# Four attention layers on one core: layers interleaved by superblocks under a build-time list scheduler

## The chip, the cores and the metric

The kernel runs on one core of a Trainium2 chip. The metric is the device time of one execution in microseconds (us), as the median of several runs. The engines are TensorE (PE in the rows; PEld is its weight load), VectorE (DVE), ScalarE (ACT), GpSimd (POOL) and SyncE (SP, which here only issues transfers).

## The reference

A sequence of 2,048 tokens of width 512 goes through four residual layers A, B, A, B. Both types have 32 heads of width 16. A is softmax attention over a sliding window of 256 keys; B is linear attention without a mask. The two A layers share their weights, and so do the two B layers.

```python
def _A_ref(x, wqkv, wo):                      # H = 32, Dh = 16, W = 256
    scores = jnp.einsum("bhqd,bhkd->bhqk", q, k) * (Dh ** -0.5)
    mask = (idx[:, None] - idx[None, :] >= 0) & (idx[:, None] - idx[None, :] < W)
    p = _softmax(jnp.where(mask[None, None], scores, -1e9), axis=-1)
    o = jnp.einsum("bhqk,bhkd->bhqd", p, v)
...
def _B_ref(x, wqkv, wo):
    phi = lambda t: jnp.where(t > 0, t + 1, jnp.exp(t)) + 1e-6
    pq, pk = phi(q), phi(k)
    kv = jnp.einsum("bhsd,bhse->bhde", pk, v)
    z = jnp.einsum("bhsd->bhd", pk)
    num = jnp.einsum("bhqd,bhde->bhqe", pq, kv)
    den = jnp.einsum("bhqd,bhd->bhq", pq, z)[..., None] + 1e-6
...
x = x + _A_ref(_layernorm(x, axis=-1), A_wqkv, A_wo)
x = x + _B_ref(_layernorm(x, axis=-1), B_wqkv, B_wo)
x = x + _A_ref(_layernorm(x, axis=-1), A_wqkv, A_wo)
x = x + _B_ref(_layernorm(x, axis=-1), B_wqkv, B_wo)
```

## The kernel before

The 2,048 tokens are 16 tiles of 128 rows, and four tiles make a superblock `I` of 512 queries. The residual `xres` stays on the chip in float32, the weights in bfloat16. `network` runs the four layers one after the other (`layer_A`, `layer_B`, each with its own PSUM pools).

**Layer A.** `prep_units` (L202) normalises a superblock's tiles: statistics on VectorE (L160, L162), the reciprocal root on GpSimd (L164, L166), the normalised tile on VectorE, ScalarE or GpSimd (L173, L178, L180), then a transpose by DMA from SP's queue (L215) or on TensorE (L186). Projections are four matmuls of 128x512 each: queries (L221), keys (L232), values (L245). The keys go to `kb` twice, with even and with odd heads masked out, so that one 32-row matmul makes the scores of a pair of heads for 64 keys; 16 pairs fill 32 heads. A row group is the quarter of TensorE's rows that a pair uses (pair modulo 4). Values go through `vst` and four small DMAs into the block-diagonal `vbd`.

`scores` (L276) treats a group of pairs (`GROUPS`: four of three pairs, two of two) and a bin of two runs of four windows (a window is 64 queries against 64 keys): matmuls (L286) into one of two PSUM buffers of three banks (`psA`), one exponential on ScalarE for up to 1,536 columns (L298), then triangular masks on GpSimd (L308) into one of nine buffers `pt`. Superblocks 1 to 3 have five bins (`BINS`), superblock 0 four (`BINS0`). `pv_pair` (L318) multiplies the masked exponentials with `vbd`, 24 matmuls of 34 columns per pair (18 in superblock 0); the 17th column of each head sums the row. `finalize` (L327, L329) divides. `outproj_units` (L268 to L272) transposes by DMA, multiplies by `wo` and adds the residual.

The order in A is written out by hand: while the scores of superblock `I` run, the projections of `I + 1` and the outputs of `I - 1` are dealt out between the score phases. Behind a layer, the row sums are tested (L387 to L393); where they are out of range, a slow version of the network runs after the fast one. It doesn't run here.

**Layer B.** For each tile LN, keys (L426), values (L432), and phi as an exponential on ScalarE and two passes on VectorE (L403 to L405); the products of keys and values of all 16 tiles add up in PSUM (`kvacc`, L441). Query projections (L447) follow per superblock. Only when all tiles are in, `kvbd` is made (L464, L466), and a second loop runs numerators and denominators (L474), the division (L478 to L481), a DMA transpose (L484), the output projection (L490) and the residual (L493, L496) for each tile.

The framework places every instruction on its engine's queue in the order of this code with some reordering by priority, and each engine works its queue in order.

Of the kernel before, what the change touches and what calls it, by code (L numbers as in the profile page):

```python
# [31 lines left out]
R1 = [(7, 7, 1), (-2, 0, 3)]  # L32
R2 = [(5, 5, 3), (-4, 0, 1)]
R3 = [(1, 1, 3), (0, 4, 1)]
R4 = [(3, 3, 3), (2, 6, 1)]
R5 = [(0, 0, 4)]
R6 = [(2, 2, 4)]
R7 = [(-1, 0, 4)]
R8 = [(4, 4, 4)]
R9 = [(-3, 0, 2), (6, 6, 2)]  # L40
R10 = [(1, 4, 2), (3, 6, 2)]
BINS = [(R3, R4), (R5, R6), (R1, R2), (R7, R8), (R9, R10)]
BINS0 = [(R3, R4), (R5, R6), (R8, R10), ([(5, 5, 3)], [(7, 7, 1), (6, 6, 2)])]
GROUPS = [(0, 1, 2), (3, 4, 5), (6, 7, 8), (9, 10, 11), (12, 13), (14, 15)]


def bin_windows(bins):

    win = {u: [] for u in range(4)}
    for b, runs in enumerate(bins):  # L50
        for r, run in enumerate(runs):
            pos = 0
            for (j, w0, n) in run:
                w = w0
                if w % 2:
                    assert pos == 0
                    win[w // 2].append((b, r, -1, j))
                    w += 1
                while w + 1 < w0 + n:
                    win[w // 2].append((b, r, pos + w - w0, j))  # L60
                    w += 2
                if w < w0 + n:
                    assert pos + w - w0 == 3
                    win[w // 2].append((b, r, pos + w - w0, j))
                pos += n
    return win


def bin_masks(runs):

    found = {}
    for r, run in enumerate(runs):
        pos = 0
        for (j, w0, n) in run:
            for w in range(w0, w0 + n):
                if w - j in (0, 4):
                    found.setdefault((w - j, pos + w - w0), []).append(r)
            pos += n
    return [(k, pos, rs) for (k, pos), rs in sorted(found.items())]
# [3 lines left out]
def build(ctx, tc, A_x, A_wqkv, A_wo, B_x, B_wqkv, B_wo, out, layers="ABAB", force_safe=False):  # L83
    nc = tc.nc
    S = A_x.shape[-2]
    NT, NSS = S // P, S // 512

# [3 lines left out]
    small = ctx.enter_context(tc.tile_pool(name="small", bufs=6))  # L91
# [34 lines left out]
    def load_weights():  # L126
        if w_loaded[0]:
            return
# [63 lines left out]
    def layer_A(x_old, x_new, w, wo, a_idx):  # L192
# [9 lines left out]
        def prep_units(I):  # L202
# [56 lines left out]
            for t in range(NCT):  # L259
                units += [qproj(t), kproj(t)]  # L260
# [410 lines left out]
```

## Time and profile before

| | us |
|---|---|
| median of 3 runs | 603.53 (601.71 to 605.83) |
| profiled execution | 602.24 |
| its span, first to last instruction | 600.2 |
| TensorE busy in it | 460.0 (77%), mean granted clock 0.892 |
| ScalarE busy | 367.5 (61%) |
| VectorE busy | 332.5 (55%) |
| GpSimd busy | 272.1 (45%) |

A busy time is the union of the instructions on an engine, so that an average over the whole span mixes stages that wait for different things. TensorE's matmuls are pipelined and their ends are modelled: the step from one start to the next tells more than a duration. The granted clock of TensorE is given as a share of 2.4 GHz; its two levels are 1.0 (2.4 GHz) and 0.5 (1.2 GHz).

### The profile page before, as it was taken

To read this page: it belongs to the slowest core of one execution; us is meant where nothing else is said; L and a number is where in the kernel's file an instruction comes from. 1 tells how busy PE (TensorE), PEld (TensorE's weight loads), DVE (VectorE), ACT (ScalarE), POOL (GpSimd) and SP (SyncE) were. 2 spreads that over 40 slices of the span, in tenths; PEclk is the share of its full clock that TensorE was granted. 3 is DMA by queue.
4 is the path that set the end of the run, shared out by engine and by line. 5 is a ranking of instruction groups with operands and counts; after the bars stand their busy time and mean duration, and the time that the engine had idled before them with its cause. 6 is when DMAs were issued, how large, how long until landed. Compare 5 with 4: busy or idle time off the path is not lost. (4 is left out here: it accounts for less than half of the span.)

```text
span 600.2 us, 15126 instructions
## 1 busy us (share of the span) xinstructions
PE 460.0 (77%) x6032; PEld 250.1 (42%) x6114; DVE 332.5 (55%) x729; ACT 367.5 (61%) x373; POOL 272.1 (45%) x667
## 2 busy tenths in 40 slices
PE   0178888888878879995647788888887887899573
PEld 0133455545546534452213345554544553444231
DVE  7731546545623365777886154554562336677773
ACT  1557679799779824660025857988978892466000
POOL 9444457657556562200035435675755666320000
PEclk9996899999976678997988779899998788999787
DMA  9412115031020030211431211501302103021363
GB/s 302 127 27 60 16 37 75 2 48 30 2 64 11 3 80 10 41 31 35 72 70 36 57 19 34 78 2 42 35 2 53 24 2 76 14 44 29 74 120 92
DMA packets 83375, 29.66 MB, mean 49 GB/s; under 512 B 67936, under 2 KB 82784, under 8 KB 83296
## 3 DMA queue, kind: packets, MB, share of 16 engines
q1 hardware_dynamic: 78256, 23.88, 19.9%
q10 hardware_dynamic: 5040, 4.72, 2.6%
q8 instruction: 50, 0.82, 0.6%
q14 instruction: 29, 0.24, 0.1%
HBM read 6.29 MB, written 2.10 MB: 14 GB/s over the span
## 5 line engine op out<-in xcount | busy, mean ns | idle before, releaser
L298 ACT ACTIVATE pt<-A 128x1536 bf16<-128x1536 f32 (+1 forms) x228 | 281.0, 1321 | 52.9 <-PE A L286 46.3
L308 POOL TENSOR_SCALAR_AFFINE_SELECT pt<-pt 128x384 bf16<-128x384 bf16 (+3 forms) x456 | 184.3, 430 | 140.1 <-ACT pt L298 136.1
L318 PE MATMUL O<-vbd,pt 128*128 128x34 bf16 x2880 | 108.4, 182 | 27.7 <-POOL pt L308 22.7
L318 PEld LDWEIGHTS <-pt 128*128 128x128 bf16 x2880 | 89.8, 99 | 64.8 <-POOL pt L308 37.9
L286 PE MATMUL A<-qT,kb 32*128 32x192 bf16 (+3 forms) x1920 | 96.7, 249 | 17.1 <-ACT pt L298 14.6
L286 PEld LDWEIGHTS <-kb 32*128 32x128 bf16 x1920 | 50.1, 98 | 69.6 <-issue 64.3
L490 PE MATMUL py<-woB,oT 128*128 128x512 bf16 x124 | 39.3, 448 | 16.6 <-DMA oT<-ob 14.1
L327 DVE RECIPROCAL rall<-O 128x24 f32<-128x24 f32 (+1 forms) x48 | 13.8, 288 | 66.7 <-PE O L318 66.7
L164 POOL TENSOR_SCALAR ln_ve<-ln_mv 128x1 f32<-128x1 f32 x64 | 14.0, 225 | 69.7 <-DVE ln_mv L162 68.2
L221 PE MATMUL pq<-xnT,wA 128*128 128x512 bf16 x108 | 37.3, 432 | 9.2 <-DVE ln_stats L160 5.6
L271 PE MATMUL py<-woA,oT 128*128 128x512 bf16 x108 | 33.1, 397 | 14.1 <-DMA oT<-o_sb 12.4
L160 DVE BATCH_NORM_STATS2 ln_stats<-xres 128x6 f32<-128x512 f32 x64 | 42.5, 681 | 0.8
L235 DVE TENSOR_SCALAR kb<-pk,mask_even 128x512 bf16<-128x512 f32 x32 | 25.3, 791 | 28.6 <-PE pk L232 24.4
L232 PE MATMUL pk<-xnT,wA 128*128 128x512 bf16 x116 | 36.5, 414 | 5.0 <-ACT kb L237 2.5
L403 ACT ACTIVATE phi_e<-pkb 128x512 bf16<-128x512 f32 x32 | 19.1, 598 | 32.9 <-PE pkb L426 31.4
L166 POOL TENSOR_TENSOR ln_rstd<-ln_ve,mhalf 128x1 f32<-128x1 f32 x64 | 36.8, 582 | 4.3 <-ACT xn L178 0.4
L226 DVE CAST qT<-pq 128x512 bf16<-128x512 f32 x24 | 16.6, 691 | 33.5 <-PE pq L221 33.4
L432 PE MATMUL pvb<-wB,xnTb 128*128 128x512 bf16 x124 | 34.8, 395 | 0.2
L426 PE MATMUL pkb<-wB,xnTb 128*128 128x512 bf16 x122 | 34.0, 396 | 0.5 <-issue 0.4
L272 DVE TENSOR_TENSOR xres<-py,xres 128x512 f32<-128x512 f32 x32 | 22.0, 686 | 21.4 <-PE py L271 20.5
L245 PE MATMUL pv<-wA,xnT 128*128 128x512 bf16 x114 | 31.9, 380 | 2.2 <-ACT kb L237 0.8
L178 ACT ACTIVATE xn<-xres,ln_nmr,ln_rstd 128x512 bf16<-128x512 f32 x12 | 9.6, 827 | 37.9 <-DVE ln_nmr L176 37.9
(71 smaller groups left out, 522.0 us busy)
## 6 DMA issues: line engine op xcount, KB each, us to landing
vbd<-vst SPq DMA_DIRECT2D x128, 34.0 KB, 1.9
out_dram<-ost ACTq DMA_DIRECT2D x16, 128.0 KB, 1.9
wB<-in_B_wqkv_dram SPq DMA_DIRECT2D x1, 1536.0 KB, 11.2
xst<-in_A_x_dram SPq DMA_DIRECT2D x8, 128.0 KB, 2.6
wA<-in_A_wqkv_dram SPq DMA_DIRECT2D x2, 512.0 KB, 7.2
xst<-in_A_x_dram ACTq DMA_DIRECT2D x8, 128.0 KB, 4.0
wA<-in_A_wqkv_dram ACTq DMA_DIRECT2D x1, 512.0 KB, 4.3
woA<-in_A_wo_dram ACTq DMA_DIRECT2D x1, 512.0 KB, 8.2
```

Of the source, the lines that this page charges most:

```text
L160: nc.vector.bn_stats(stats[:], x_ap)
L166: nc.gpsimd.tensor_tensor(rstd[:], ve[:], mhalf[:], op=ALU.pow)
L221: nc.tensor.matmul(pq[:], lhsT=w[:, c, t * P:(t + 1) * P], rhs=xnTs[I][:, c, :], start=(c == 0), stop=(c == NCT - 1))
L232: nc.tensor.matmul(pk[:], lhsT=w[:, c, D + t * P:D + (t + 1) * P], rhs=xnTs[I][:, c, :], start=(c == 0), stop=(c == NCT - 1))
L271: nc.tensor.matmul(py[:], lhsT=oT[:, c, :], rhs=wo[:, c, :], start=(c == 0), stop=(c == NCT - 1))
L286: nc.tensor.matmul(A[:, g, r, pos:pos + n, :], lhsT=kbs[m // 8][32 * rg:32 * rg + 32, t, m % 8, :, :], rhs=qTs[I][32 * rg:32 * rg + 32, t, ...
L298: nc.scalar.activation(body[:, 0:2 * ng, 0:n, :], A[:, 0:ng, :, 0:n, :].rearrange("p g r s c -> p (g r) s c"), ACT.Exp, scale=0.25)
L308: nc.gpsimd.affine_select(out=v, in_=v, compare_op=ALU.is_ge, fill=0.0, base=1 if kind == 0 else -2, pattern=[[0, nx], [2 * s, 64]], chann ...
L318: nc.tensor.matmul(O[:, u, g, :, :], lhsT=PTs[b][:, s0:s0 + 2, :], rhs=vbd[(m // 8) % NV][:, m % 8, :, grp[g], :], start=(n == 0), stop=(n ...
L426: nc.tensor.matmul(pk[:], lhsT=xnT[:, c, u * P:(u + 1) * P], rhs=w[:, c, D:2 * D], start=(c == 0), stop=(c == NCT - 1))
L432: nc.tensor.matmul(pv[:], lhsT=xnT[:, c, u * P:(u + 1) * P], rhs=w[:, c, 2 * D:3 * D], start=(c == 0), stop=(c == NCT - 1))
L490: nc.tensor.matmul(py[:], lhsT=oT[:, c, :], rhs=wo[:, c, :], start=(c == 0), stop=(c == NCT - 1))
```

## The change

`layer_A`, `layer_B` and the hand-written order go. In their place `fast_network` describes all operations of all four layers to a `Planner`, each with an assumed cost per engine, what it reads and writes, the buffers it takes from rings, and a priority. `Planner.run` then walks through an assumed time at build: it picks again and again the operation that can start first (with a bias on some second engine, and a higher priority where starts are equal), puts it on that engine and emits its instructions. The result is a fixed order of each engine's queue. Evictions from PSUM, masks and normalisations may go to either of two engines.

The layers are interleaved by superblocks: as soon as superblock `I` of A is out, LN, key, value and query projections and the key-value sums of B for it may run, beside A's attention of the later superblocks; the sums are now added in SBUF by VectorE, tile pairs at a time (`kv_unit`). Behind the last superblock `kv_final` masks the sums; B's second half for superblock `I` is then followed by the next A of that superblock. Denominators get a matmul group and one reciprocal of their own for four tiles (`den_unit`).

Runs of windows are longer: five runs of eight windows instead of ten of four, so that a run is a whole bank. Score phases alternate between one buffer of three banks and one of two; the other three banks (`psM`, two before) serve all other matmuls. Groups are five of three pairs and one of a single pair. The `pt` buffers are five of each size. Masks may run as a multiplication with a triangle (`tri`) on VectorE. The key eviction writes both masked copies in one instruction per half. `x` is read from the loaded bfloat16 tile without a cast. Transposes go through TensorE in the first superblock, around the layers' ends and for every second tile of the last stage, and by DMA from SP's queue elsewhere. The stores of the result move from ScalarE's queue to SP's. The slow version gets its own layer B.

```diff
-BINS = [(R3, R4), (R5, R6), (R1, R2), (R7, R8), (R9, R10)]
-BINS0 = [(R3, R4), (R5, R6), (R8, R10), ([(5, 5, 3)], [(7, 7, 1), (6, 6, 2)])]
-GROUPS = [(0, 1, 2), (3, 4, 5), (6, 7, 8), (9, 10, 11), (12, 13), (14, 15)]
...
+RA = [(1, 1, 5), (-3, 0, 2), (-4, 0, 1)]
+RB = [(3, 3, 5), (-2, 0, 3)]
+RC = [(-1, 0, 4), (4, 4, 4)]
+RD = [(5, 5, 3), (0, 0, 5)]
+RE = [(7, 7, 1), (6, 6, 2), (2, 2, 5)]
+
+BINS = ([RA, RE, RB], [RD, RC])
+BINS0 = ([RD, RE], [[(1, 1, 5), (4, 4, 2)], [(3, 3, 5), (4, 6, 2)]])
+GROUPS = [(0, 1, 2), (3, 4, 5), (6, 7, 8), (9, 10, 11), (12, 13, 14), (15,)]
...
+def phases_of(bins):
+
+    n3, n2 = len(bins[0]), len(bins[1])
+    out = []
+    for grp in GROUPS:
+        u3 = [(b, p) for b in range(n3) for p in grp]
+        u2 = [(b, p) for b in range(n3, n3 + n2) for p in grp]
+        while u3 or u2:
+            for us, n in ((u3, 3), (u2, 2)):
+                if us:
+                    out.append((n, us[:n]))
+                    del us[:n]
+    return out
...
+        n = 0
+        while ready:
+            best = None
+            for o, t in ready.items():
+                ok = True
+                for s in o.takes:
+                    f = s.ring.free_at()
+                    if f is None:
+                        ok = False
+                        break
+                    t = max(t, f[0])
+                if not ok:
+                    continue
+                for e, c in o.cost.items():
+                    c, bias = c if isinstance(c, tuple) else (c, 0.0)
+                    start = max(t, free[e])
+                    key = (round(start + bias, 2), o.prio, o.n)
+
+                    if best is None or key < best[0]:
+                        best = (key, o, e, start, c)
...
+                if not is_warm(start):
+                    c *= {"scores": 1.6, "pv": 1.28}.get(o.kind, 2.0)
...
+            o.fn(e)
...
+        ps3 = pool("ps3", 1, space=PSUM)
+        ps2 = pool("ps2", 1, space=PSUM)
+        psM = pool("psM", 3, space=PSUM)
...
+        rings = {"M": Ring(3), "3": Ring(1), "2": Ring(1), "xnT": Ring(3), "xn": Ring(4), "oT": Ring(4), "ost": Ring(3),
+                 "phi": Ring(2), "pks": Ring(3), "vs": Ring(3), "ln": Ring(8), "rden": Ring(2)}
...
+            return pl.op({"DVE": .69, "ACT": (.6, actb)}, fn, EV, reads=reads, writes=writes, deps=deps, use=[take_slot] + list(use))
...
+            ap = pl.op({"DVE": .45} if first else {"POOL": 1.0, "DVE": (.6, 0.0 if fast else .8)}, f_ap, prio, reads=[B("x", i)],
...
+            mm = pl.op({"PE": .33}, f_mm, prio, reads=reads, deps=lastmm + list(bPT.r), take=[s], kind="scores")
...
+                        pc = .18 + .064 * c if y - x == 1 else len(ps) * (.18 + .064 * 1.25 * (y - x))
+                        o = pl.op({"POOL": pc, "DVE": (.1 + .064 * .75 * c, .3)}, f_m, prio, deps=[exo])
...
+                def fe(e, jj=jj, t=t):
+                    if i == 0:
+                        nc.vector.tensor_copy(kvs[jj][:], t["t"][:])
+                    else:
+                        nc.vector.tensor_tensor(kvs[jj][:], t["t"][:], kvs[jj][:], op=ALU.add)
+                pl.op({"DVE": .42}, fe, EV, deps=[o], use=[s], writes=[B("kvs", jj)])
...
+        for k in range(NH):
+            nc.gpsimd.memset(vbd[k][:], 0.0)
+        for k in range(NPT):
+            nc.gpsimd.memset(pts[3][k][:, 0:28:9, :], 0.0)
+            nc.gpsimd.memset(pts[2][k][:, 0:19:9, :], 0.0)
...
+        def prep(key, I, prio, actb=ACTB):
+            for t in range(NCT):
+                k_unit(key, I, t, prio)
+                q_unit(key, I, t, prio, actb)
+            for u in range(4):
+                v_unit(key, I, u, prio, actb)
+
+        def b_proj(key, I, prio, actb=ACTB):
+            for u in range(4):
+                bk_unit(key, 4 * I + u, prio)
+                bv_unit(key, 4 * I + u, prio, actb)
+                if u % 2:
+                    kv_unit(4 * I + u - 1, prio)
+            for t in range(NCT):
+                bq_unit(key, I, t, prio + .5)
+
+        for a in range(2):
+            for I in range(NI):
+                ka, kb_ = ("A", a, I), ("B", a, I)
+                lastI = I == NI - 1
+                if a == 1:
+                    R = den_unit(I, 1.5 if I < 2 else 2.5)
+                    for u in range(4):
+                        p2_tile(4 * I + u, R, 1.5 if I < 2 else 2.5, by_pe=I < 2, actb=0.0 if I < 2 else ACTB)
+                for u in range(4):
+                    ln_tile(ka, 4 * I + u, a == 0, 2, by_pe=(I == 0 or (a == 1 and I == 1)), actb=0.0 if I == 0 else ACTB, fast=I == 0)
+                prep(ka, I, 2.2, actb=0.0 if I == 0 else ACTB)
+                attention(I, 0)
+                out_A(I, a, 1.6 if lastI else 3, by_pe=lastI, actb=0.0 if lastI else ACTB)
+                for u in range(4):
+                    ln_tile(kb_, 4 * I + u, False, 1.6 if lastI else 3.2, by_pe=lastI, actb=0.0 if lastI else ACTB, fast=lastI)
+                b_proj(kb_, I, 1.8 if lastI else 4, actb=0.0 if lastI else ACTB)
+            kv_final(0)
+            check_sums(a)
+        for I in range(NI):
+            R = den_unit(I, 2)
+            for u in range(4):
+                p2_tile(4 * I + u, R, 2, by_pe=True if u % 2 == 0 else False, final=True, actb=0.0)
+        late_consts()
+        plan_log = []
+        with tc.manual_schedule():
+            span = pl.run(plan_log)
```

## Rows read from the trace of the kernel before

**Rows 1.** The page's first part: busy time, share of the span, instructions.

```profile
PE 460.0 (77%) x6032; PEld 250.1 (42%) x6114; DVE 332.5 (55%) x729; ACT 367.5 (61%) x373; POOL 272.1 (45%) x667
```

**Rows 2.** Windows by stage: length; busy of PE, PEld, DVE, ACT, POOL; clock, DMA.

```profile
0.00:41.10 41.10, 11.18 (x63) 5.12 (x65) 28.41 (x65) 15.19 (x24) 26.30 (x55) 1.00 0.54 166
41.10:211.20 170.10, 141.53 (x2519) 83.49 (x2550) 75.67 (x145) 143.69 (x122) 99.13 (x249) 0.88 0.16 31
211.20:326.70 115.50, 89.04 (x491) 41.20 (x500) 85.05 (x209) 36.22 (x60) 30.03 (x73) 0.88 0.25 49
326.70:497.10 170.40, 140.92 (x2519) 83.28 (x2550) 75.56 (x145) 143.89 (x122) 99.05 (x249) 0.88 0.17 31
497.10:600.20 103.10, 77.32 (x444) 36.99 (x451) 67.82 (x165) 28.56 (x48) 17.64 (x41) 0.90 0.31 65
```

**Rows 3.** Windows: two within the first attention, one within layer B's projections.

```profile
80.00:120.00 40.00, 33.73 (x657) 20.28 (x664) 22.11 (x44) 35.59 (x30) 26.22 (x64) 1.00 0.25 42
160.00:211.20 51.20, 42.49 (x809) 26.68 (x815) 17.61 (x36) 44.91 (x38) 30.30 (x81) 0.73 0.10 23
...
240.00:256.00 16.00, 15.89 (x88) 7.90 (x89) 11.52 (x24) 10.06 (x17) 3.55 (x9) 1.00 0.21 42
```

**Rows 4.** Waits, whole span: engine and line, released by; us in total, times, longest.

```profile
ACT pt L298 <- PE A L286: 46.3, 57, 4.4
...
PE O L318 <- POOL pt L308: 22.7, 35, 2.5
```

**Rows 5.** Groups by shape: exponentials, masks; busy us, mean ns, idle before by releaser.

```profile
L298 ACT ACTIVATE pt<-A 128x1536 bf16<-128x1536 f32 x144 | 198.7, 1488 | 21.3 <-PE A L286 17.4 <-POOL pt L308 3.8
...
L298 ACT ACTIVATE pt<-A 128x1024 bf16<-128x1024 f32 x72 | 71.9, 1033 | 21.6 <-PE A L286 20.1 <-POOL pt L308 1.3
...
L308 POOL TENSOR_SCALAR_AFFINE_SELECT pt<-pt 128x192 bf16<-128x192 bf16 x128 | 43.8, 357 | 38.2 <-ACT pt L298 36.8 <-PE py L271 1.4
...
L308 POOL TENSOR_SCALAR_AFFINE_SELECT pt<-pt 128x128 bf16<-128x128 bf16 x64 | 17.9, 294 | 15.4 <-ACT pt L298 15.4
```

**Rows 6.** Timeline in attention: start us, duration, engine, line, operation, count.

```profile
101.02 0.40 PE L286 MATMUL A<-qT,kb 32*128 32x256 bf16 x6
...
101.34 0.67 PEld L318 LDWEIGHTS <-pt 128*128 128x128 bf16 x24 [0.21 <-issue]
```

**Rows 7.** Timeline in layer B: two projections in a row.

```profile
259.12 1.02 PE L426 MATMUL pkb<-wB,xnTb 128*128 128x512 bf16 x4
...
259.98 1.03 PE L432 MATMUL pvb<-wB,xnTb 128*128 128x512 bf16 x4
```

**Rows 8.** Groups by shape: LN, transposed eviction, residual and phi's exponential.

```profile
L160 DVE BATCH_NORM_STATS2 ln_stats<-xres 128x6 f32<-128x512 f32 x64 | 42.5, 681 | 0.8
...
L166 POOL TENSOR_TENSOR ln_rstd<-ln_ve,mhalf 128x1 f32<-128x1 f32 x64 | 36.8, 582 | 4.3 <-ACT xn L178 0.4
...
L272 DVE TENSOR_TENSOR xres<-py,xres 128x512 f32<-128x512 f32 x32 | 22.0, 686 | 21.4 <-PE py L271 20.5 <-PE A L286 0.9
...
L403 ACT ACTIVATE phi_e<-pkb 128x512 bf16<-128x512 f32 x32 | 19.1, 598 | 32.9 <-PE pkb L426 31.4 <-PE kvacc L441 1.0 <-DVE pks L405 0.5
...
L164 POOL TENSOR_SCALAR ln_ve<-ln_mv 128x1 f32<-128x1 f32 x64 | 14.0, 225 | 69.7 <-DVE ln_mv L162 68.2 <-DVE vint L622 1.1
L173 DVE TENSOR_SCALAR xn<-xres,ln_mv,ln_rstd 128x512 bf16<-128x512 f32 x24 | 13.6, 567 | 18.6 <-DMA xnT<-xn 16.1 <-POOL pt L308 1.2 <-PE pT L186 1.1
...
L190 DVE COPY xnTb<-pT 128x512 bf16<-128x512 bf16 x4 | 1.6, 393 | 1.5 <-PE pT L186 1.5
```

**Rows 9.** One line's instructions: count, least/median/greatest ns, first and last start.

```profile
L404 DVE TENSOR_SCALAR phi_e<-phi_e x64: 260/294/709, 217.3 to 555.7; 128x512 bf16<-128x512 bf16 x64
...
L180 POOL TENSOR_SCALAR xn<-xres,ln_rstd,ln_nmr x28: 772/772/1284, 108.9 to 540.3; 128x512 bf16<-128x512 f32 x28
```

**Rows 10.** Group of the zeroing of vbd; timeline of SP's queue in the last stage.

```profile
L153 POOL MEMSET vbd<- 128x2176 bf16 x4 | 7.6, 1910 | 0.0
...
559.08 32.00 SPq L484 DMA_TRANSPOSE oT<-ob  x16
```

More of the change, by code (lines that the diff above doesn't have):

```diff
@@ L66, in bin_windows @@
[L66 to L72, printed above, removed]
+    for b, run in enumerate(bins):
         pos = 0
         for (j, w0, n) in run:
[L75 to L79 removed]
+            w = w0
+            if w % 2:
+                assert pos == 0
+                win[w // 2].append((b, -1, j))
+                w += 1
+            while w + 1 < w0 + n:
+                win[w // 2].append((b, pos + w - w0, j))
+                w += 2
+            if w < w0 + n:
+                assert pos + w - w0 == 7
+                win[w // 2].append((b, pos + w - w0, j))
+            pos += n
@@ new lines, in bin_windows, with bin_masks @@
+    return win
+def bin_masks(run):
+    found = {}
+    pos = 0
+    for (j, w0, n) in run:
+        for w in range(w0, w0 + n):
+            if w - j in (0, 4):
+                found.setdefault(w - j, []).append(pos + w - w0)
+        pos += n
+    return {k: tuple(v) for k, v in found.items()}
+def phases_of(bins):
[10 more added lines that the diff above has]
+    return out
@@ new lines, with __init__, free_at @@
+class Buf:
+    def __init__(self):
+        self.w, self.r = [], []
+class Ring:
+    def __init__(self, n):
+        self.n, self.tiles = n, [None] * n
+    def free_at(self):
+        b = [(0.0 if t is None else t.end + .1, k) for k, t in enumerate(self.tiles) if t is None or not t.left]
+        return min(b, default=None)
+class Slot:
+    def __init__(self, ring):
+        self.ring, self.users, self.left, self.end = ring, [], 0, 0.0
+class Op:
+    def __init__(self, n, cost, fn, prio, kind):
+        self.n, self.cost, self.fn, self.prio, self.kind = n, cost, fn, prio, kind
+        self.deps, self.slots, self.takes = set(), [], []
+        self.after = 0.0
+        self.end = None
@@ L183, in pe_transpose @@
-    def pe_transpose(dst, src, pool, tag, use_act=False):
-        pT = pool.tile([P, NCT, P], BF, name="pT", tag=tag)
+    vflags = consts.tile([1, 2], F32, name="vflags")
+    nc.vector.memset(vflags[:], 1.0)
+    tri = {k: consts.tile([P, 64], BF, name=f"tri{k}") for k in (0, 4)}
+    for k, t in tri.items():
+        nc.gpsimd.memset(t[:], 1.0)
+        nc.gpsimd.affine_select(out=t[:], in_=t[:], compare_op=ALU.is_ge, fill=0.0, base=1 if k == 0 else -2,
+                                pattern=[[2 if k == 0 else -2, 64]], channel_multiplier=-1 if k == 0 else 1)
@@ new lines, in safe_network @@
+    def safe_network():
+        with ExitStack() as ctx_l:
+            sx = ctx_l.enter_context(tc.tile_pool(name="sx", bufs=2))
+            for i in range(NT):
+                xst = sx.tile([P, D], BF, name="xst_s", tag="xst_s")
+                nc.sync.dma_start(xst[:], x_dram[i])
+                nc.vector.tensor_copy(xres[:, i, :], xst[:])
+        for li in range(4):
+            with ExitStack() as ctx_l:
+                if li % 2 == 0:
+                    layer_A_safe(ctx_l, xres, xres, wA, woA)
+                else:
+                    layer_B_safe(ctx_l, xres, xres, wB, woB, li == 3)
```

1032 lines of the change are left out of this document (607 added, 425 removed).

## The prediction

> **What bounds the kernel now.** The page's busy line comes first: no engine is above 77% and ScalarE, VectorE and GpSimd lie between 45% and 61% [rows 1]. Nothing is full over the whole, so the span has to be cut into stages. I cut it where the exponentials of line 298 begin and end; the table of windows then shows five stretches [rows 2]: 41.1 us before the first exponential, two attention stretches of 170.1 and 170.4 us, 115.5 us between them (layer B, then the projections of the second layer A) and 103.1 us behind them (the second B). Attention is 340.5 us, everything else 259.7 us.
>
> In attention ScalarE is the engine to watch: 143.7 of 170.1 us, 84%. In an inner window at granted clock 1.00 it is 35.59 of 40 us, 89%, with TensorE at 33.73 [rows 3]. What ends its waits is the score matmul (46.3 us in both stretches), while TensorE's PV matmuls wait for GpSimd's masks (22.7 us) [rows 4]. In the non-attention stretches ScalarE is nearly idle (36.2 of 115.5 us) and TensorE does 89.0 us of work, dense only in places: 15.89 of 16 us in the projections of B [rows 2, 3]. Two stage types with different bounds run one after the other; the change runs B's projections under A's exponentials.
>
> **The change part by part.** *Exponentials.* The columns stay: 16 pairs x (30 + 3 x 40) windows x 64 = 153,600 a layer. The instructions go from 114 to 123 a layer: 58 of 1,536 columns, 49 of 1,024, 16 of 896. Busy time per instruction is 198.7/144 = 1.38 and 71.9/72 = 1.00 us [rows 5]; with 0.90 taken for 896 that is 80.0 + 49.0 + 14.4 = 143.4 us a layer, 3 us more than now.
>
> *Scores.* 123 phases a layer instead of 114. A phase of 1,536 columns starts at 101.02 and the PV behind it at 101.34: 0.32 us, for three pairs side by side [rows 6]; where a projection needs 0.86 us for 4 x 512 columns, 0.215 each [rows 7]. The last group has now one pair, whose units share a row group and so run one after another: 8 phases, some 2.3 us more in all by 0.215 per 512 columns. 123 x 0.33 + 2.3 = 42.9 us a layer.
>
> *PV.* Still 24 matmuls per pair (18 in superblock 0), 1,440 a layer; 24 weight loads took 0.67 us [rows 6], 0.028 each: 40.3 us.
>
> *Projections.* 256 in all, as before, at 0.86. What counts is where they fall. Between the first and the last exponential of the first A: 10 left of superblock 0, 36 of superblocks 1 to 3, 12 outputs, and 36 of B for superblocks 0 to 2: 94 x 0.86 = 80.8 us; K-V sums 12 x 0.24 = 2.9 (four matmuls of 129 columns against four of 512). Sum of TensorE: 42.9 + 40.3 + 80.8 + 2.9 = 166.9 us. In the second A also the 12 outputs of B for superblocks 1 to 3, their numerators (2.9), denominators (about 1.4, 48 matmuls priced as PV) and 8 tiles transposed on TensorE (2.4 at 0.3): 106 x 0.86 + 2.9 + 6.7 + 83.2 = 184.0 us. So TensorE, not ScalarE, has the largest sum in attention (ScalarE: 143.4 + 24 exponentials of phi at 0.60 = 157.8, and some evictions that the planner gives it).
>
> *VectorE and GpSimd.* Masks keep their columns but are cut into 424 instead of 228 instructions a layer on GpSimd: 200 of 192 columns at 0.34, 136 of 128 at 0.28, 88 of 64 at 0.22 (the line through the other two): 125.7 us against 92.2 now [rows 5]. With 24 tiles of statistics (0.22 + 0.58) and 24 normalisations (1.0 with the added negation) GpSimd would need 169 us, so the planner moves masks to VectorE. VectorE's own work in the second stretch, with every pass over 512 columns of PSUM priced as the residual, 0.69, and shorter ones in proportion [rows 8, 9]: 24 x 0.88 statistics (0.68 and a short aggregate taken as 0.2), 14 x 1.38 keys, 26 x 0.69 queries and values, 24 x 0.74 finalize, 24 x 0.69 residuals, 24 x 0.98 phi, 12 x 0.69 values of B, 12 x 0.35 for the K-V adds that PSUM did before, 12 x 0.69 numerators and some 7 more: 144 us. Together 313, 157 each; in the first stretch, without B's second half, 146 each; less if ScalarE takes evictions. Removed: 16 casts of x, a scalar operation per LN on VectorE, 36 of 120 DMA transposes (44 tiles go through TensorE, 8 did). On SP's queue stay 84 transposes, at up to 2.0 us [rows 10] 168 of 521 us, the 128 value copies and, new, the 16 stores: hidden in total, but in order, so that a transpose behind a value copy that waits for its eviction arrives late, and the projections of that superblock after it; TensorE then has PV and another superblock's projections to do.
>
> *How full can the stretch be?* This decides. The upper bound is the 99% that TensorE reaches alone in B, the lower the 84% of ScalarE over the whole attention stretch [rows 2, 3]. The stretch stays an attention stretch, so it is nearer to the lower; but the last third of it now ran at granted clock 0.73 with few projections [rows 3], and there B's projections fill in. I take 0.90: 166.9/0.90 = 185.4 and 184.0/0.90 = 204.4 us.
>
> *Start.* GpSimd's memsets stand ahead of its first LN: five of `vbd` at 1.91 us [rows 10] and some 6 us of smaller ones, so the first rstd is near 17 us; four tiles of it, normalisation, transposes, projection (0.86, twice that at the low clock), eviction and scores give some 25 us where it was 41.1.
>
> *Middle.* From the last exponential to the first of the next layer nothing of attention can run: output of superblock 3, LN, B's projections, K-V sum, then superblock 0 through B's output, LN and the projections. VectorE paces it: 0.39 + 0.69 + 0.88 + 0.57 + 0.39 + 0.98 = 3.9 us a tile [rows 8, 9], four tiles 15.6, with the first tile's steps on other engines (two projections, a rstd, an exponential, two transposes: some 6.5) and PV ahead (2.3) 24.4; K-V sum and its masking 1.6; second half 4 x 3.6 = 14.4 and 5.1 for the steps elsewhere; first key projection to exponential 2.5: 48 us instead of 115.5.
>
> *Tail.* The same 26 us to the masked K-V sum, then 16 tiles x 1.6 us on VectorE (0.69 + 0.69 + half of 0.39) = 25.6, last tile and store 6: 58 us instead of 103.1. Now 16 DMA transposes in a row take 32.0 us there, 2.0 each [rows 10]; half of them go to TensorE.
>
> Sum: 25 + 185.4 + 48 + 204.4 + 58 = 521 us of span. The profiled execution had 602.24 us for a span of 600.2, 2 us around it, and the median of the runs is 1.3 us above that execution: 524, rounded to 525.
>
> **The rivals.** *A, the plan packs tighter.* With TensorE at 0.98 as in B, the stretches are 170 and 188 and the sum 25 + 358 + 48 + 58 + 3 = 492; middle and tail a tenth shorter give 481. For it: there is always projection work waiting. Against: each eviction must free one of three PSUM buffers, and a score phase arriving during a projection waits up to 0.86 us.
>
> *B, VectorE and GpSimd block each other.* The first phi operation on VectorE takes 0.29 us, but 0.71 at most, and GpSimd's normalisation 0.77, but 1.28 at most [rows 9]; I read the long ones as one engine waiting for the other. That is rare now because GpSimd is idle in most of B [rows 2]; afterwards phi, VectorE's masks and LN all run beside GpSimd's masks. By 0.42 us for some 24 phi, 12 LN and 40 masks a stretch each engine would gain 32 us: 146 + 32 = 178 and 157 + 32 = 189, over 0.90 198 and 210 us, more than TensorE's, sum 198 + 210 + 131 + 3 = 542; with half as many such meetings again 577. The Trainium skill's page "SBUF — State Buffer", section "SBUF: two separate sides", says that an instruction of VectorE which uses both ports, or reads two SBUF inputs against a reading GpSimd, and one of GpSimd exclude each other for a whole instruction; by that the masks on VectorE (two SBUF inputs) would be held up too and the time would be this rival's. The two maxima in the trace agree with it; how often it happens, no row shows.
>
> *C, no overlap.* In-order queues could leave B's work behind A's: stretches as now (340), start 25, middle 105, tail 95: 568. Against it speaks that B's projections need only LN of finished superblocks.
>
> *D, slower.* Score buffers: now two of three banks each, then one of three banks and one of two. If every score phase had to wait out a projection, ScalarE would idle 0.86 us per exponential: 2 x 123 x (1.17 + 0.86) = 499 + 131 + 3 = 633. It decides from 0.74 us per exponential on (469 us of attention for 603 in all). Against: the wait now is 46.3/228 = 0.2 us with projections in the same queue [rows 4], and the exponential from the other buffer (1.0 or 1.38 us) covers most of one.
>
> **How the numbers follow.** Forecast (500 to 550) 0.45, A (below 500) 0.21, B (550 to 577) 0.16, C 0.09, D 0.05, and 0.04 for a mixture that ends within 1% of 603.5, which is about what a measurement of this kernel can tell from no change. A, the forecast, B and C are faster by over 1%: 0.91; same 0.04; slower 0.05. The range runs from A's lower end, 481, to just beyond C, 572; it leaves out D, the mixture and the edges of A and B.
>
> **What would show it.** Exponentials must be spread over two stretches of 185 and 205 us, with B's phi exponentials inside them; TensorE above 85% busy there with granted clock near 1.0; first exponential near 25 us; 48 us without exponentials in the middle, 58 behind. B shows as phi operations of 0.5 us and more, and PV waiting for masks; D as ScalarE waiting for scores over 100 us; C as phi after the last exponential. I am wrong if attention stretches exceed 230 us or the middle exceeds 70.

## The result and the profile after

The median went from 602.62 us (601.37 to 605.83) to 562.54 us (560.12 to 565.3): 0.9329 of the time before, 95% interval 0.9267 to 0.939. The profiled execution has a span of 559.5 us at a mean granted clock of 0.928. The forecast was 525, in a range of 481 to 572.

The page's busy line, against [rows 1]; TensorE's work is the same to 7 us, and the span around it is 41 us shorter:

```profile
PE 467.1 (83%) x5828; PEld 240.0 (43%) x5906; DVE 385.8 (69%) x912; ACT 348.7 (62%) x365; POOL 281.4 (50%) x871
```

The windows by stage, cut as in [rows 2] (here the exponentials are line 534; length, then busy time of PE, PEld, DVE, ACT, POOL, clock, DMA share, GB/s):

```profile
0.00:25.30 25.30, 9.03 (x44) 4.07 (x45) 10.42 (x30) 3.56 (x6) 17.50 (x39) 1.00 0.64 213
25.30:231.20 205.90, 179.73 (x2507) 92.14 (x2539) 138.17 (x351) 158.57 (x158) 114.94 (x373) 0.91 0.18 40
231.20:286.60 55.40, 41.98 (x321) 21.65 (x323) 44.66 (x96) 15.62 (x27) 22.19 (x54) 0.92 0.00 1
286.60:475.60 189.00, 173.58 (x2527) 90.68 (x2558) 132.77 (x318) 151.24 (x143) 118.53 (x383) 0.97 0.21 42
475.60:559.50 83.90, 62.78 (x447) 31.42 (x451) 59.74 (x121) 19.74 (x34) 8.27 (x24) 0.87 0.15 39
```

Set beside the forecast, the sum is off by 38.5 us, and it is made of misses of both signs:

| stage | forecast | changed kernel | difference |
|---|---|---|---|
| start | 25 | 25.3 | 0.3 |
| first attention stretch | 185.4 | 205.9 | 20.5 |
| middle | 48 | 55.4 | 7.4 |
| second attention stretch | 204.4 | 189.0 | -15.4 |
| tail | 58 | 83.9 | 25.9 |

**The first stretch** is not short of work everywhere. Within it, three places have a TensorE that stands still, and a low clock beside it; the 40 us from 105 on are full:

```profile
38.00:48.00 10.00, 3.76 (x56) 2.23 (x56) 1.98 (x3) 0.00 (x0) 0.00 (x0) 0.56 0.36 96
48.00:65.00 17.00, 16.16 (x225) 8.32 (x226) 13.98 (x35) 13.57 (x15) 10.42 (x34) 0.96 0.17 37
65.00:85.00 20.00, 15.80 (x183) 7.81 (x185) 11.32 (x26) 10.85 (x10) 9.14 (x32) 0.71 0.20 54
...
105.00:145.00 40.00, 39.30 (x607) 20.61 (x614) 26.14 (x66) 34.79 (x32) 25.57 (x85) 0.97 0.14 31
145.00:165.00 20.00, 16.81 (x234) 8.18 (x236) 12.66 (x33) 13.48 (x15) 12.48 (x37) 0.83 0.19 44
```

The share of TensorE's time in use and its granted clock are low together in these places. From 38 to 48 us neither ScalarE nor GpSimd does anything. The waits of 38 to 50 us (engine and line, released by; total, times, longest) name a transfer, and the timeline of SyncE's queue shows what it stood behind:

```profile
ACT pt L534 <- PE A L516: 11.5, 2, 11.3
...
PEld L587 <- DMA vbd<-vst: 8.1, 2, 5.1
DVE vst L359 <- DMA vbd<-vst: 4.7, 1, 4.7
```

```profile
34.09 2.53 SPq L382 DMA_TRANSPOSE xnT<-xn  x2
36.72 2.45 SPq L492 DMA_DIRECT2D vbd<-vst  x4
39.27 1.22 SPq L382 DMA_TRANSPOSE xnT<-xn  x1
40.59 5.24 SPq L492 DMA_DIRECT2D vbd<-vst  x8
45.87 1.06 SPq L266 DMA_DIRECT2D xres<-in_A_x_dram  x2
...
63.26 5.03 SPq L492 DMA_DIRECT2D vbd<-vst  x8
68.33 1.06 SPq L266 DMA_DIRECT2D xres<-in_A_x_dram  x2
...
139.26 5.86 SPq L492 DMA_DIRECT2D vbd<-vst  x8
145.16 2.58 SPq L382 DMA_TRANSPOSE oT<-o_sb  x2
```

TensorE's timeline behind the third place (in brackets the idle time before, and what ended it):

```profile
149.70 1.86 PE L372 MATMUL ps<-woA,oT 128*128 128x512 bf16 x4 [2.92 <-DVE o_sb L602]
```

The queue is busy without a gap from 34 to 47 us. The four value copies of one tile take 2.45 us to issue; the planner's list gives them 0.4. PV of the first superblock waits for `vbd`, the scores behind PV in TensorE's order wait with it, and the exponentials wait for the scores for 11.3 us. The next hole has the same form: the last load of `x` stands behind eight copies and starts at 68.33, VectorE's statistics wait 4.05 us for it, an eviction of values stands behind them on VectorE, and a projection waits 3.46 us for that. So has the third: two transposes of attention's output start at 145.16, behind eight copies; VectorE waits 4.36 us until they have read the buffer that it writes next, and a projection 2.92 us for VectorE. At 293.72 sixteen such copies in a row stand for 10 us at the same place of the second layer.

**The tail** begins with projections that do not belong there. All 12 query projections of B for superblocks 0 to 2 fell into the first stretch in the first layer; in the second layer the stretch has none, and the tail has all 16 units, four matmuls each (groups by shape of line 372, first the first stretch, then the tail; 48 and 64 matmuls ran, of which the trace recorded 44 and 62):

```profile
L372 PE MATMUL ps<-xnT,wB 128*128 128x512 bf16 x44 | 12.1, 379 | 0.5 <-DVE pks L660 0.3
...
L372 PE MATMUL ps<-xnT,wB 128*128 128x512 bf16 x62 | 15.1, 378 | 0.7 <-DVE xres L454 0.3 <-DVE pqT L660 0.2
```

Behind them come the numerators, in four rounds of four tiles, cut here at the denominators of each round:

```profile
475.60:512.00 36.40, 31.37 (x229) 15.81 (x230) 31.26 (x71) 17.40 (x30) 8.27 (x24) 1.00 0.00 1
512.00:524.40 12.40, 9.35 (x55) 4.57 (x55) 7.47 (x17) 0.59 (x1) 0.00 (x0) 0.59 0.18 46
524.40:533.00 8.60, 6.03 (x57) 3.32 (x57) 6.72 (x11) 0.59 (x1) 0.00 (x0) 1.00 0.29 76
533.00:544.80 11.80, 8.64 (x58) 3.93 (x58) 6.75 (x12) 0.59 (x1) 0.00 (x0) 0.71 0.35 79
544.80:559.50 14.70, 7.40 (x56) 3.79 (x55) 7.55 (x12) 0.59 (x1) 0.00 (x0) 0.83 0.27 76
```

VectorE needs about 7 us a round, the rounds take 8.6 to 14.7.

**The middle.** From the masked K-V sum at 258.6 to the first exponential, VectorE's groups hold eight tiles of LN statistics and of divided numerators where the forecast had four, and two denominators that it did not have (line, busy us, mean ns):

```profile
L412 DVE BATCH_NORM_STATS2 ln_st<-xres 128x6 f32<-128x512 f32 x8 | 5.5, 688 | 0.2
L760 DVE TENSOR_TENSOR ob<-pn,rden 128x512 bf16<-128x512 f32 x8 | 5.3, 679 | 0.2 <-DVE rden L744 0.2
...
L744 DVE RECIPROCAL rden<-rden 128x128 f32<-128x128 f32 x2 | 1.9, 954 | 0.1
```

### The profile page after: what moved, and what is told of

Its sections match the earlier page's. It is cut to its first block, busy times and chain, and to the rows that moved or that the text cites. A ratio compares the mean times of both kernels' runs of the same rounds, so it can differ in the third digit from the quotient of the medians.

```text
span 559.5 us, 14879 instructions
## 1 busy us (share of the span) xinstructions
PE 467.1 (83%) x5828; PEld 240.0 (43%) x5906; DVE 385.8 (69%) x912; ACT 348.7 (62%) x365; POOL 281.4 (50%) x871
## 3 DMA queue, kind: packets, MB, share of 16 engines
q1 hardware_dynamic: 62032, 22.30, 17.4%
## 4 chain that ended last, share of the span: by engine, by line
PE 64%; DVE 14%; DMA 5%; POOL 5%; issue 4%; ACT 3%; SPq 3%; DVEq 0%; ACTq 0%; POOLq 0%
PE ps L372 36%; PE A L516 13%; PE O L587 12%; SPq L492 3%; DMA oT<-ob 3%; ACT pt L534 2%; DVE pqT L660 2%; POOL vbd L351 2%; DVE ln_st L412 2%; DVE xres L454 1%; PE pT L391 1%; DVE rden L744 1%; DVE ob L760 1%; PE pkv L703 1%; DMA vbd<-vst 1%
## 5 line engine op out<-in xcount | busy, mean ns | idle before, releaser
L534 ACT ACTIVATE pt<-A 128x1536 bf16<-128x1536 f32 (+2 forms) x246 | 286.1, 1214 | 71.4 <-PE A L516 39.2
L561 POOL TENSOR_SCALAR_AFFINE_SELECT pt<-pt 128x192 bf16<-128x192 bf16 (+2 forms) x600 | 175.3, 325 | 131.6 <-ACT pt L534 128.6
L516 PE MATMUL A<-qT,kbd 32*128 32x320 bf16 (+4 forms) x1440 | 104.6, 262 | 4.8 <-ACT pt L534 4.4
L372 PE MATMUL ps<-xnT,wA 128*128 128x512 bf16 x235 | 68.5, 406 | 14.4 <-ACT pt L534 4.3
L372 PE MATMUL ps<-wB,xnT 128*128 128x512 bf16 x237 | 63.1, 380 | 2.4 <-DVE o_sb L602 0.4
L556 DVE TENSOR_TENSOR pt<-pt,tri 128x64 bf16<-128x64 bf16 (+4 forms) x217 | 52.3, 267 | 16.2 <-ACT pt L534 15.6
L473 DVE TENSOR_TENSOR kbd<-ps,eo 128x512 bf16<-128x512 f32 x64 | 41.3, 684 | 22.9 <-PE ps L372 20.8
L656 ACT ACTIVATE phi_e<-ps 128x512 bf16<-128x512 f32 x64 | 38.3, 598 | 24.2 <-PE ps L372 22.2
L412 DVE BATCH_NORM_STATS2 ln_st<-xres 128x6 f32<-128x512 f32 (+1 forms) x64 | 43.9, 685 | 7.4 <-DMA xres<-in_A_x_dram 6.9
L372 PE MATMUL ps<-woB,oT 128*128 128x512 bf16 x117 | 39.5, 473 | 7.6 <-DMA oT<-ob 4.6
L454 DVE TENSOR_TENSOR xres<-ps,xres 128x512 f32<-128x512 f32 x48 | 32.6, 682 | 13.6 <-PE ps L372 12.7
```

The costliest lines, as they stand in the source:

```text
L372: nc.tensor.matmul(t["t"][:], lhsT=lhs(c), rhs=rhs(c), start=(c == 0), stop=(c == NCT - 1))
L412: nc.vector.bn_stats(t["st"][:], x())
L454: nc.vector.tensor_tensor(xres[:, i, :], ps()[:], x0(i) if first else xres[:, i, :], op=ALU.add)
L473: nc.vector.tensor_tensor(kbd[r][:, t, :, :, :].rearrange("p m k h -> p (m k) h"), ps()[:, hf * 256:(hf + 1) * 256].unsqueeze(2).to_broadc ...
L516: nc.tensor.matmul(A[:, x, at[x]:at[x] + w, :], lhsT=kbd[half(m)][32 * rg:32 * rg + 32, tt, m % 4, :, :], rhs=qT[I % 2][32 * rg:32 * rg + ...
L534: nc.scalar.activation(body[:, x:y, 0:pos[x], :], t["A"][:, x:y, 0:pos[x], :], ACT.Exp, scale=0.25)
```

## The experiments

Each one is compared with the kernel before, run beside it; the ratio of the changed kernel to that is 0.9329. Theory: SyncE's in-order queue holds up the stretches, and two things of the plan, late queries and shared PSUM banks, lengthen the tail. Rivals: TensorE is full and the queue is hidden; VectorE and GpSimd block each other (rival B); the overlap is not what gives the gain (rival C).

### Value copies issued twice

```diff
 nc.sync.dma_start(vbd[half(m)][h::2, m % 4, h, :, :], vst[n][64 * mb:64 * mb + 64, h, :, :])
+nc.sync.dma_start(vdum[64 * mb:64 * mb + 64, h, :, :], vst[n][64 * mb:64 * mb + 64, h, 0:NP // 2, :])
```

> Each of the four value copies of a tile is issued a second time, half as wide, into a scratch tile that nobody reads; the order of every other engine is the same as in the changed kernel. Theory 'SyncE queue' (the 20 us that the first stretch has over the forecast come from SyncE's in-order queue, where the four value copies take 2.45 us a tile): the issue time per tile about doubles, 32 x 2.45 = 78 us more in the queue; four tiles in a row make the first PV or the next transpose of a superblock 5 to 10 us later, in seven superblocks: 590 us (575 to 615), the first stretch 220 to 235 us instead of 205.8. Rival 'TensorE is full and the queue is hidden': within 1% of the changed kernel, 557 to 568.

Measured: 627.8 us, 1.0346 (1.0283 to 1.0408). The windows of both stretches:

```profile
25.90:264.40 238.50, 187.05 (x2540) 93.50 (x2539) 137.25 (x351) 158.81 (x158) 115.11 (x373) 0.85 0.19 39
...
322.30:545.10 222.80, 184.45 (x2559) 92.60 (x2558) 132.70 (x318) 151.60 (x143) 117.98 (x383) 0.89 0.21 40
```

They are 32.6 and 33.8 us longer, middle and tail about as before (57.9 and 81.6 us). Of some 78 us more in the queue, 65 come out at the end (62 by the two ratios, 67 in the spans). It is above the theory's range, and the hidden queue falls: in the attention stretches most of what is added to SyncE's queue is paid. Not all of it is the order of the queue alone: the added copies also hold the two `vst` buffers until they have landed, and evictions into these wait for them, 27.3 us on VectorE and 15.5 on ScalarE. A third `vst` buffer was not tried, so that the two are not told apart in this run.

### Half of the value copies from ScalarE's queue, then all of them

```diff
-nc.sync.dma_start(vbd[half(m)][h::2, m % 4, h, :, :], vst[n][64 * mb:64 * mb + 64, h, :, :])
+(nc.sync if h == 0 else nc.scalar).dma_start(vbd[half(m)][h::2, m % 4, h, :, :], vst[n][64 * mb:64 * mb + 64, h, :, :])
```

> Two of the four value copies of a tile are issued from ScalarE's queue instead of SyncE's; the planned order is the same. Theory 'SyncE queue': 32 x 1.2 = 39 us leave the queue, the first stretch loses 5 to 10 of its 205.8 us, the second 2 to 6: 550 us (545 to 558). Against it works that ScalarE's instructions wait behind the issue (64 issues; two loads of x took 2.6 us there). Rival 'the queue is hidden': 557 to 575, no gain and perhaps a loss from ScalarE.

Measured: 539.9 us, 0.8935 (0.8869 to 0.9001).

```profile
25.60:216.40 190.80, 176.69 (x2539) 90.89 (x2537) 138.21 (x351) 158.46 (x158) 115.00 (x373) 0.95 0.21 43
...
274.10:456.60 182.50, 175.24 (x2559) 90.53 (x2558) 132.76 (x318) 151.16 (x143) 118.02 (x383) 0.98 0.23 43
```

The order of the work is the same, and 15.1 and 6.5 us are gone from the two stretches, with the clock up from 0.91 to 0.95 in the first. The total gain, 23 us, is about twice what was expected; the direction and the place are the theory's.

> All four value copies of a tile on ScalarE's queue, none on SyncE's. Theory 'SyncE queue', that only SyncE's load counts: another 39 us leave SyncE, 532 us (525 to 537). Rival 'issue time is a cost wherever it stands': 128 issues at 0.54 us are 70 us in ScalarE's queue, the exponentials behind them come later and 540 to 560 results, no better than with half of the copies (539.9).

Measured: 564.1 us, 0.9353 (0.9278 to 0.9428), with all four copies on `nc.scalar`. The waits show why (ScalarE's exponentials, released by):

```profile
ACT pt L534 <- DMA vbd<-vst: 33.4, 16, 4.3
```

ScalarE's queue pays 0.61 us per copy (median of 128) in front of exponentials. So the rival of this run holds, and the time is even above its range (540 to 560): issue time costs where the queue is needed, and the gain lies in dividing it.

### Score banks in the tail; the late queries left out

```diff
+        def bank(k):
+            if not big:
+                big[3] = ps3.tile([P, 3, 512], F32, name="T3", tag="A3_0", bufs=1)
+                big[2] = ps2.tile([P, 2, 512], F32, name="T2", tag="A2_0", bufs=1)
+            return big[3][:, k, :] if k < 3 else big[2][:, k - 3, :]
...
-            s, rs = slot("M"), slot("rden")
+            s, rs = slot("X" if final else "M"), slot("rden")
...
-            s, xs = slot("M"), slot("xn")
+            s, xs = slot("X" if final else "M"), slot("xn")
```

> In the last stage the numerators and denominators use the five PSUM banks of the score buffers, which are idle then, and leave the three banks of psM to transposes and output projections. The order up to the last exponential is the same. Theory 'the tail's four rounds follow one another because three banks are shared': the 46.6 us behind 512.9 shrink to 35 (32 to 40), the total by 8 to 13 us: 552 (548 to 556). Rival 'DMA transposes or the lower clock pace the tail': 560 to 565.

Measured: 555.2 us, 0.9156 (0.9093 to 0.9219). The last stage is 75.7 us long instead of 83.9:

```profile
477.20:552.90 75.70, 58.65 (x453) 30.32 (x449) 57.84 (x117) 22.09 (x38) 8.24 (x24) 0.93 0.16 44
```

> The second layer B's query projections of superblocks 0 to 2 (12 of 0.86 us, with their phi) are left out, so that the result differs. Theory 'they were put off past the last exponential and lengthen the tail': the tail loses 10 to 13 of its 84 us, the two stretches stay within 2 us: 551 (547 to 555). Rival 'hidden under VectorE in the tail': 560 to 565.

Measured: 550.3 us, 0.9077 (0.9018 to 0.9135), edit: `bq_unit` only in the first layer B and for superblock 3. The last stage is 13.0 us shorter, the second stretch 2.0 us longer:

```profile
477.80:548.70 70.90, 50.73 (x409) 26.37 (x405) 49.08 (x96) 13.87 (x24) 7.65 (x22) 0.89 0.17 46
```

Both times lie in the ranges that the theories gave, the first one at its edge: the total fell by 7.3 us where 8 to 13 were expected. What remains of the tail above the forecast after both, if they add, is some 5 us; that sum was not run by itself (e8_q_early below has both, with other work moved into the tail).

### No overlap

```diff
...
-                for u in range(4):
-                    ln_tile(kb_, 4 * I + u, False, 1.6 if lastI else 3.2, by_pe=lastI, actb=0.0 if lastI else ACTB, fast=lastI)
-                b_proj(kb_, I, 1.8 if lastI else 4, actb=0.0 if lastI else ACTB)
+            last = [o for o in pl.ops if o.kind == "exp"][-1:]
+            for I in range(NI):
+                for u in range(4):
+                    ln_tile(("B", a, I), 4 * I + u, False, 1.6, by_pe=True, actb=0.0, fast=True, wait=last)
+                b_proj(("B", a, I), I, 1.8, actb=0.0)
...
```

Left out here: B's second half of the first layer B moves ahead of the second A, whose LN waits for its last residual.

> Everything of the change stays, but layer B's LN waits for the last exponential of its A, and the second A's LN for the last residual of B's second half; so no projection of B can run beside A's exponentials, and the planner packs each layer alone. Theory 'the gain comes from B's work inside the attention stretches': slower than the kernel before, 640 us (615 to 660), the stretches near 175 each and the middle above 125. Rival C's reading, 'the gain comes from the rest (start, tail, PSUM split, transposes)': 568 (555 to 590).

Measured: 636.5 us, 1.0558 (1.0462 to 1.0653).

```profile
24.20:208.90 184.70, 154.34 (x2348) 82.76 (x2347) 101.37 (x270) 144.62 (x130) 90.10 (x287) 0.81 0.16 36
208.90:342.30 133.40, 103.28 (x706) 53.22 (x703) 100.74 (x219) 48.41 (x84) 40.15 (x101) 0.90 0.02 4
342.30:512.00 169.70, 151.63 (x2343) 81.17 (x2342) 94.26 (x250) 143.21 (x127) 91.42 (x286) 0.83 0.13 28
512.00:632.60 120.60, 92.26 (x611) 46.41 (x607) 85.78 (x183) 41.69 (x72) 25.30 (x69) 0.90 0.10 28
```

Against [rows 2] the start is 17 us shorter, but the middle and the tail are each about 18 us longer and the first stretch 15: layer B by itself is slower in the new form. The time lies in the theory's range, and rival C's reading falls: between this kernel and the changed one lie 74 us (636.5 to 562.5), and without the overlap the change would lose 34 against before. Some of the 74 can be the other transposes and priorities of this experiment, so that they are an upper bound for the overlap.

### The combined kernel, early queries, the true price

> Half of the value copies on ScalarE's queue, numerators and denominators of the last stage in the score banks, and all 16 transposes of the last stage on TensorE. Theory: the first two gains add (23 and 7 us), and with the DMA transposes gone the tail is another 0 to 4 us shorter: 530 us (526 to 535), the tail 70 to 75. Rival 'the two gains overlap': 537 to 541.

Measured: 533.0 us, 0.8822 (0.8743 to 0.8901). The first two gains add, to within 1 us; the last stage is 73.4 us where half of the copies alone had 80.6. The share of the TensorE transposes in it is too small to be told.

```diff
-                bq_unit(key, I, t, prio + .5)
+                bq_unit(key, I, t, prio - .3)
```

> As the combined kernel, but the query projections of layer B get a higher priority than its keys and values, so that they are not put off past the last exponential. Theory 'TensorE is full in the second stretch, a projection costs the same wherever it stands': the second stretch 8 to 12 us longer, the tail 9 to 13 shorter, the total within 4 us of the combined kernel. Rival 'the tail's projections are the dearer ones, since the stretch has holes': 6 to 12 us faster.

Measured: 529.1 us, 0.8766 (0.8696 to 0.8836). The 12 units are back in the second stretch. Its groups of line 372 for layer B, first the queries, then keys and values in e7_combined and keys and values here:

```profile
L372 PE MATMUL ps<-xnT,wB 128*128 128x512 bf16 x48 | 12.1, 380 | 0.0
...
L372 PE MATMUL ps<-wB,xnT 128*128 128x512 bf16 x96 | 24.8, 380 | 0.5 <-DVE kvs L708 0.3 <-DVE o_sb L602 0.2
...
L372 PE MATMUL ps<-wB,xnT 128*128 128x512 bf16 x74 | 19.0, 380 | 0.3 <-DVE kvs L710 0.3
```

That stretch went from 182.6 to 188.2 us and the tail from 73.4 to 68.4: both about half of what the theory had. The lines show why: 12 units of queries came in, and about six units of keys and values went out into the tail in their place (the tail has 56 such matmuls for 32), so that the net is six units, 5.2 us at 0.86. TensorE is full there, as the theory said; what it missed is that something else gives way. The total is as it said, 3.9 us less; the two intervals overlap, so that a gain is not shown. In the profiles the difference lies in the middle, 54.1 us for 57.5 at a clock of 0.97 for 0.88, and why it is there stays open.

```diff
-            pl.op({"SP": .4}, fd, prio, reads=[B("vst", n)], writes=[B("v", half(m0), (m0 % 4) // 2)])
+            pl.op({"SP": 1.2}, fd, prio, reads=[B("vst", n)], writes=[B("v", half(m0), (m0 % 4) // 2)])
```

> As e8_q_early, and the planner is told what the two value copies of a tile cost on SyncE's queue, 1.2 us instead of 0.4; nothing else changes but the order that follows. Theory 'a better price gives a better order on the chip': 522 to 527. Rival 'the order only becomes another one, since the plan's own assumed end goes from 515 to 518 us and its other prices err as well': 527 to 537.

Measured: 522.1 us, 0.8605 (0.8554 to 0.8656), clear of the one before. The first stretch fell from 192.2 to 184.7 us and the tail from 68.4 to 64.8, while the second stretch grew from 188.2 to 192.9. The planner's own end became later by 3 us and the chip's earlier by 7: here the assumed time was no measure of the order that it makes.

### Copies from GpSimd's queue; masks on GpSimd alone

> As e8_q_early, but the half of the value copies that ScalarE's queue issues there is issued by GpSimd's queue; the planned order is the same. Theory 'issue time costs where the queue is needed, and GpSimd has the most idle time (284 of 528 us busy)': 524 to 529. Rival 'GpSimd's issue is dearer than 0.54 us, masks behind it come late, PV waits': 533 to 560.

Measured: 521.9 us, 0.8632 (0.8582 to 0.8681), better than either side expected and clear of e8_q_early (against e8_q_early `nc.scalar` became `nc.gpsimd`). The line's instructions (least/median/greatest ns) show what GpSimd pays, and its busy time rose from 283.8 to 315.3 us without a loss:

```profile
L492 SPq DMA_DIRECT2D vbd<-vst x64: 461/547/1952, 21.2 to 391.4; - x64
L492 POOL DMA_DIRECT2D vbd<-vst x64: 516/525/752, 21.4 to 391.1; - x64
```

> As e8_q_early, but every mask runs on GpSimd, none on VectorE (217 did). Theory 'VectorE and GpSimd do not hold each other up noticeably; only the balance changes': GpSimd gets some 70 us more, VectorE 37 less, PV waits more for masks: 546 us (538 to 555), phi's first operation stays at its median of 0.29 us. Rival B, 'masks on VectorE and masks on GpSimd block each other': taking one of them away costs nothing, 525 to 533, and the long phi operations (0.5 us and more) disappear.

Measured: 550.9 us, 0.9113 (0.9068 to 0.9158), with `{"POOL": pc}` as the masks' only price, so that the planner has no other engine for them. First its phi operation, then the wait of the division for PV (17.4 us in 28 times in e8_q_early):

```profile
L659 DVE TENSOR_SCALAR phi_e<-phi_e x64: 260/294/614, 114.0 to 509.5; 128x512 bf16<-128x512 bf16 x64
```

```profile
DVE rall L601 <- PE O L587: 37.2, 30, 9.1
```

Phi's median stays and its longest stays above 0.5 us, while some 21 us are lost. The masks on VectorE are worth their place. The time lies in the range of the first theory. The planner's order changes with this price as well, so that a small gain from fewer meetings of the two engines is not ruled out by it.

### All of it

> As e10_copies_gpsimd, with the true price of SyncE's two copies told to the planner as in e9_true_price. Theory 'the two steps act on different things (which queue carries the copies, in which order everything stands) and add': 514 us (510 to 519). Rival 'both take out the same waits': 519 to 525, no better than either alone.

Measured: 518.1 us (514.8 to 520.0), 0.8551 (0.8515 to 0.8588), the fastest of this study: 0.917 of the changed kernel's ratio. The time lies in the theory's range, but alone the two steps gave 7.0 and 7.3 us and together 11.0, so they add only in part, and the intervals overlap those of e9_true_price and e10_copies_gpsimd: that the two add is not shown.

```profile
24.50:207.10 182.60, 173.75 (x2511) 88.75 (x2509) 135.66 (x339) 158.16 (x158) 130.77 (x402) 0.97 0.24 45
...
263.20:450.00 186.80, 182.60 (x2628) 94.73 (x2629) 147.49 (x343) 156.22 (x153) 132.03 (x406) 0.99 0.21 42
450.00:515.10 65.10, 50.02 (x413) 27.23 (x411) 47.51 (x95) 19.94 (x35) 8.86 (x28) 0.92 0.10 35
```

## Why the prediction was right and wrong

**Right: direction and mechanism.** The gain comes from B's projections under A's exponentials; without the overlap the kernel is slower than before. Phi's exponentials run inside the stretches, 24 of 64 in the first and 12 in the second, so C falls:

```profile
L656 ACT ACTIVATE phi_e<-ps 128x512 bf16<-128x512 f32 x24 | 14.4, 601 | 3.5 <-PE ps L372 2.6 <-DVE pt L556 0.5
```

The first exponential came at 25.3 us for 25, which is partly luck: the first rstd came at 14.8 us instead of 17, and the steps behind it took 10.5 us instead of 8. The total, 562.5 us, lies in the stated range but outside the forecast's own band (500 to 550), in the one given to rival B by a mechanism that the runs don't show.

**Wrong: SyncE's queue priced at nothing.** The step "hidden in total, but in order ... TensorE then has PV and another superblock's projections to do" named the wait and dropped it. What was missing is the value copies' issue price, which no row in front shows beside the transposes [rows 10]: 0.59 us each, 2.45 us a tile, in front of transposes, `x` and other copies. The trace of the kernel before had it, and there, in the order written by hand, PV's matmuls waited only 2.8 us in all for these copies, and their weight loads 2.2. The transposes were priced too high: 2.0 us each was the pace of a row with waits in it, and the instruction took 1.19 us in the median (least/median/greatest ns):

```profile
L256 SPq DMA_DIRECT2D vbd<-vst x128: 461/594/1815, 45.1 to 461.5; - x128
...
L484 SPq DMA_TRANSPOSE oT<-ob x32: 1188/1190/1916, 274.8 to 589.9; - x32
```

So copies and transposes together, 183 us, came near the 168 us that the prediction gave to the transposes alone; what failed is the place in time, bursts of copies in front of a first consumer. And TensorE's order is fixed as well: when PV stands first and waits, the projections behind it, ready or not, wait too. That is what 38 to 48 us show. The term's size, from the two runs on both sides: 78 us more in the queue cost 62 to 65 us (with the `vst` buffers), 39 us less gave 23.

The Trainium skill's page "DMA: Bandwidth & Descriptors", section "Issuing engines are not separate DMA queues", says that starting DMAs from several engines saves only the sequencer's time to start them, usually small beside the DMA. The trace agrees that it is the time to start that is saved, since the time to landing stayed (1.9 us, and 2.0 with half of the copies moved); small it is not here: starting took 0.59 us against 1.9 us to landing, and dividing it saved 23 us.

**Wrong by compensation: "I take 0.90" for both stretches.** It was 0.87 of TensorE in the first, with the queue's holes, and 0.92 in the second, with 10 us of queries fewer than summed. The first stretch's 20.5 us are for the larger part the sum itself: TensorE was busy for 179.7 us there, at a clock of 0.91, where the terms gave 166.9. At 0.90 that is 14 us, and the fill adds 6. In e12_best, at 0.97, it was still 173.8, so some 7 us are missing from the terms; the other 6 fit the lower clock. Which term is short stays open. In the second stretch the terms were right: 184.0 less 10.3 of queries is 173.7, and 173.6 were measured. That the two stretches together miss by 5 us only is luck. With the queue relieved and the queries back, TensorE is at 0.95 and 0.98, close to the 0.99 of B alone [rows 3]: rival A's price for the stretches, 358 us, was nearer (369 measured) than the forecast's 390. Why the fill was limited was wrong too: not the mix of stage types, but one queue.

**Wrong: the tail, 25.9 us.** Half of it is placement: I put 36 projections of B per layer inside the stretch since they could run there, but the change gives the queries the lowest priority, `prio + .5`, and the second stretch had no room for them (13.0 us when left out; 5.0 when moved back, where keys and values went out in their place). The rest is the term 16 x 1.6 us on VectorE: it left out four denominators on VectorE (0.28 + 0.95 us each, 5 us) and took the rounds as overlapping, though three shared banks keep them apart (8.2 us when five more are given).

**Wrong: the middle, 7.4 us.** The first half was right, 27.4 us for 26.0, with the row-sum test's 1.8 us on VectorE left out. The second half took 28.0 for 22: VectorE, busy for 24.5 of them, had the tiles of superblock 1 as well before the first exponential. Superblocks 0 and 1 share a priority there; that this is the reason was not tested.

**Rival B.** Phi's first operation has nearly the same times as before (0.29 us in the median, 0.76 at most; in front 0.29 and 0.71 [rows 9]), and GpSimd's masks of 192 columns take 371 ns in the mean for 357 [rows 5]:

```profile
L659 DVE TENSOR_SCALAR phi_e<-phi_e x64: 260/294/761, 119.8 to 511.8; 128x512 bf16<-128x512 bf16 x64
```

With every mask on GpSimd some 21 us were lost, where blocking would have made them free. The rule quoted there, the lock in the Trainium skill's page "SBUF — State Buffer", section "SBUF: two separate sides", may hold for single instructions, which no run here shows or rules out; the loss of 32 us an engine that the rival worked out isn't there. **Rival D.** ScalarE waits for scores 39.2 us in all, less than the 46.3 of [rows 4]; 11.3 of them are the one stall behind `vbd`.

The forecast's 525 us is close to what the plan can do once the queue is mended (518 to 529), which is no merit of the sum: its tail was too short and its stretches too long.

## What to carry to other kernels

Price every instruction of an issuing queue from its own row, small copies first, and add them up in order at the point where a first consumer waits; a queue that is busy for a third of the span (here 128 copies at 0.61 and 84 transposes at 1.26 us in the mean, 183 of 559.5) can still lengthen it. When a scheduler fixes each engine's order, one late transfer stops all that is queued behind its consumer, so a price that is too low in its list can be a stall on the chip (0.4 us to 1.2 gave 7 us here). Look where low-priority work ends up, since full stretches push it behind the end.

## What the runs showed of the hardware

The same small copy costs 0.55 to 0.59 us of issue on SyncE, 0.54 to 0.61 on ScalarE and 0.53 on GpSimd (medians), each in the order of that engine's work; SyncE's DMA transposes cost 1.20 to 1.22 us.

A stall costs more than its length. With the copies doubled, TensorE's busy time for the same matmuls of the first stretch was 187.1 us at a mean granted clock of 0.85; with half of them moved it was 176.7 at 0.95. In the changed kernel the clock was 0.56, near the lower of its two levels (1.2 GHz), while TensorE waited from 38 to 48 us, and it was 0.96 in the 17 us behind it. The first projection of four matmuls behind the three holes took 1.87, 1.87 and 1.86 us; in a full stretch, from 156 us on, it is 1.04.
